# Attention outputs summed transposed on eight 64x32 tiles, expert weights in halves, and a reordered opening

## Chip, cores, metric

The kernel runs on one core of one Trainium2 chip. The metric is the device time of an execution in microseconds (us), given as the median of several executions. Each run belongs to a state (fast or slow, by its time against the fastest run of the same kernel), and comparisons here use fast runs unless a sentence says otherwise. A profile covers one execution; its span is some 1.7 us shorter than the device time.

PE is the tensor engine, PEld its weight loads, DVE the vector engine, ACT the scalar engine, POOL the general engine, SP the one that issues most transfers. PEclk is the clock granted to PE.

## The reference, cut to what matters

```python
def _attn_ref(r, k, v, w, u):                 # (4, 8, 768, 48): batch, heads, time, channels
    state = np.zeros((B, H, D, D))
    for t in range(S):
        cur = np.einsum('bhd,bhe->bhde', u[None] * kt, vt)
        y[:, :, t] = np.einsum('bhd,bhde->bhe', rt, state + cur)
        state = w[None, :, :, None] * state + np.einsum('bhd,bhe->bhde', kt, vt)

def _moe_ref(x, w_gate, w1, w2):              # x: (4, 768, 384), 8 experts, F = 1024
    logits = x.mean(axis=1) @ w_gate          # one expert for a whole sequence
    e_idx = np.argmax(logits, axis=1)
    ...
        h = np.maximum(x[mask] @ w1[e], 0.0)
        out[mask] = gate_w[mask, None, None] * (h @ w2[e])
```

A linear attention with a decaying state comes first. Its output, averaged over a sequence, chooses one expert for the sequence, so no expert work of a sequence can start before the attention of the whole sequence is done.

## The kernel before

Time is cut into blocks of 256 steps: three blocks a sequence, twelve in all (0 to 11). Within a block, scores are products of k and r, and outputs are products of masked scores (`gt`) and values (`vb`). Expert work is a queue of jobs (`hp` and `op` products), and `slot()` puts some of them between the pieces of attention. The opening does blocks 0 to 2 without expert work; the loop does blocks 3 to 11 with jobs of the sequence before.

The products that the change touches, in the shape they have before:

```python
# scores: four 64x64 tiles, 16 products for half of a block
nc.tensor.matmul(out=at[64 * j : 64 * j + 64, a, pp, cs, :],
                 lhsT=kt[q, p, j, cs, :], rhs=rt[q, p, j]..., start=True, stop=True)
...
# outputs: time on the partitions, one product of 48 columns for each head and half
nc.tensor.matmul(out=yj[:, D * h : D * h + D],
                 lhsT=gt[q, p // 2, a, p % 2, c, :], rhs=vb[q, c, h, :], ...)
...
def backs(g):     # outputs are copied, transposed back, and copied again; column sums for the gate
    nc.tensor.transpose(out=xv[:, ct, :, j, :], in_=xn[:, j, ct::NCT], identity=ident)
    nc.tensor.matmul(out=sp[:, o : o + 1], lhsT=xn[:, j, ct::NCT], rhs=ones_col, ...)
    nc.scalar.copy(xts[b][:, :, L * gi : L * gi + L], xp)
...
def weights(b):   # all of w1 in one transfer, then w2, when the gate has chosen
    nc.gpsimd.dma_start(out=w1..., in_=moe_w1[ds(ev, 1)]...)
```

The whole kernel:

## Time and profile before

| | before |
|---|---|
| time, median of the first three runs | 154.54 us (153.83 to 156.16) |
| span of the profiled run | 152.6 us |
| PE busy | 91% of the span |
| first gate logits (`lg`) | 33.1 us |
| first expert matmul (`hp`) | 45.0 us |

The prediction below shows the engine shares, the slices and the chain. Two lines that it did not look at also belong here. They are from the page's part on transfer queues; the columns are packets, MB, and share of the sixteen transfer engines' time:

```profile
q0 software_dynamic: 1152, 6.29, 22.3%
q8 instruction: 15, 0.25, 0.6%
```

I read queue 8 as PE's own program, by its packet count: 15 packets of 16 KB for the 3913 PE instructions of the trace, 261 to a packet. Queue 0 carries the expert weights.

### The profile page before, as it was taken

How to read it: one execution, taken by the hardware profiler on the slowest of the kernel's cores; microseconds unless marked ns; L12 is line 12 of the kernel's file. 1: busy time of each engine (PE TensorE's matmuls, PEld its weight loads, DVE VectorE, ACT ScalarE, POOL GpSimd, SP SyncE). 2: the span in 40 equal slices, each digit the busy share in tenths (PEclk: the TensorE clock that was granted, in tenths of full speed). 3: DMA queues.
4: the chain of work that ended last, by engine and by line, in shares of the span. 5: the costliest groups of instructions: out<-in, count | busy, mean ns of one | idle time of the engine just before them, and what ended most of it. 6: DMA issues, size and time to landing. Idle time of an engine off the chain costs nothing.

```text
span 152.6 us, 4539 instructions
## 1 busy us (share of the span) xinstructions
PE 139.5 (91%) x1951; PEld 97.9 (64%) x1951; DVE 74.4 (49%) x164; ACT 83.6 (55%) x144; POOL 68.5 (45%) x62
## 2 busy tenths in 40 slices
PE   6999877956989999999999999999999999999991
PEld 2266645644767878766677877666777765676560
DVE  7837796125465654754548456465562321121110
ACT  0976567351356766546476784563664543556231
POOL 4169659207976839289292862963021020000000
PEclk9999999995599999999999999999999999999999
DMA  2999998303999999999991000998020079960034
GB/s 59 301 322 321 279 268 226 99 0 92 227 215 297 249 312 269 293 214 210 215 376 48 4 0 4 153 195 267 22 93 4 0 111 208 161 247 0 0 126 185
DMA packets 41464, 25.47 MB, mean 167 GB/s; under 512 B 38755, under 2 KB 39012, under 8 KB 41444
## 3 DMA queue, kind: packets, MB, share of 16 engines
q1 hardware_dynamic: 39460, 18.89, 42.9%
q0 software_dynamic: 1152, 6.29, 22.3%
q8 instruction: 15, 0.25, 0.6%
q10 hardware_dynamic: 832, 0.00, 0.3%
q14 instruction: 5, 0.04, 0.1%
HBM read 26.76 MB, written 4.72 MB: 206 GB/s over the span
## 4 chain that ended last, share of the span: by engine, by line
PE 78%; DVE 10%; ACT 8%; issue 2%; DVEq 0%
PE op L503 21%; PE hp L483 21%; PE twp L236 7%; PE at L260 5%; DVE gt L268 5%; PE fill L113 5%; PE y L353 5%; ACT kr L246 4%; PE s L361 2%; PE xp L402 2%; ACT ht L490 2%; PE y L313 2%; PE y L323 2%; DVE ht L492 1%; DVE st L376 1%
## 5 line engine op out<-in xcount | busy, mean ns | idle before, releaser
L483 PE MATMUL hp<-xt,w 128*128 128x384 bf16 x192 | 41.4, 334 | 1.3 <-DVE lg L436 0.3
L503 PE MATMUL op<-w,ht 128*128 128x384 bf16 x192 | 34.9, 326 | 0.1
L246 ACT COPY kr<-twp 128x1024 bf16<-128x1024 bf16 x24 | 24.1, 1011 | 18.4 <-PE twp L236 18.4
L268 DVE TENSOR_TENSOR gt<-at,mask 128x1024 bf16<-128x1024 f32 x24 | 29.3, 1221 | 8.8 <-PE at L260 8.6
L490 ACT ACTIVATE ht<-hp 128x384 bf16<-128x384 f32 x48 | 23.4, 491 | 17.8 <-PE hp L483 17.1
L483 PEld LDWEIGHTS <-w 128*128 128x128 bf16 x192 | 25.0, 148 | 8.1 <-issue 4.4
L305 POOL TENSOR_TENSOR vt<-vb,tcol 128x768 bf16<-128x768 bf16 x11 | 16.3, 1477 | 25.4 <-DVE tcol L297 25.4
L503 PEld LDWEIGHTS <-ht 128*128 128x128 bf16 x192 | 17.3, 97 | 11.1 <-issue 0.8
L247 DVE TENSOR_TENSOR prod<-twp,kr 128x512 bf16<-128x512 bf16 x24 | 10.2, 424 | 27.8 <-ACT kr L246 27.8
L199 POOL TENSOR_TENSOR kp<-k,dk 128x768 bf16<-128x768 f32 x11 | 20.0, 1816 | 1.4 <-DMA k<-in_k_dram 1.4
L199 POOL TENSOR_TENSOR rp<-r,dr 128x768 bf16<-128x768 f32 x11 | 20.0, 1820 | 0.0
L510 ACT ACTIVATE ob<-op,gw 128x384 f32<-128x384 f32 x16 | 9.3, 581 | 13.2 <-PE op L503 12.9
L113 PE MATMUL fill<-zero 128*128 128x512 bf16 (+1 forms) x45 | 14.5, 430 | 1.9 <-DVE zero L85 1.3
L353 PEld LDWEIGHTS <-gt 64*128 64x128 bf16 x384 | 11.5, 94 | 5.0 <-issue 3.9
L492 DVE TENSOR_SCALAR ht<-hp 128x384 bf16<-128x384 f32 x16 | 8.9, 554 | 11.7 <-PE hp L483 11.5
L353 PE MATMUL y<-vb,gt 64*128 64x48 bf16 x384 | 14.1, 182 | 0.4 <-ACT xn L389 0.4
L260 PE MATMUL at<-kr 48*64 48x128 bf16 x384 | 10.5, 229 | 3.6 <-ACT kr L246 1.7
L389 ACT CAST xn<-y 128x384 bf16<-128x384 f32 x24 | 11.1, 480 | 4.1 <-PE y L323 3.5
L462 POOL DMA_DIRECT2D w<-in_moe_w_dram x4 | 2.5, 623 | 22.5 <-DVE gw L452 7.8
L260 PEld LDWEIGHTS <-kr 48*64 48x64 bf16 x384 | 7.0, 110 | 8.2 <-issue 6.2
L410 ACT COPY xt<-xp 128x768 bf16<-128x768 bf16 x12 | 9.6, 798 | 4.3 <-PE xp L402 4.3
L361 PE MATMUL s<-vb,kp 64*128 64x96 bf16 x160 | 10.5, 208 | 0.4 <-DVE st L376 0.4
(73 smaller groups left out, 155.6 us busy)
## 6 DMA issues: line engine op xcount, KB each, us to landing
w<-in_moe_w_dram POOLq DMA_DIRECT2D x8, 768.0 KB, 10.2
k<-in_k_dram SPq DMA_DIRECT2D x12, 384.0 KB, 5.1
r<-in_r_dram SPq DMA_DIRECT2D x12, 384.0 KB, 5.8
v<-in_v_dram SPq DMA_DIRECT2D x12, 384.0 KB, 5.7
out_dram<-ob SPq DMA_DIRECT2D x11, 384.0 KB, 5.6
out_dram<-ob SPq DMA_DIRECT2D x2, 192.0 KB, 1.9
wuT<-in_w_dram ACTq DMA_DIRECT2D x2, 0.8 KB, 3.6
wuT<-in_u_dram ACTq DMA_DIRECT2D x2, 0.8 KB, 4.1
```

The source lines that it names most:

```text
L113: nc.tensor.matmul(out=fills[-1][:, 0:cols], lhsT=zero[:, 0:128], rhs=zero[:, 0:cols], start=True, stop=True)
L199: eng.tensor_mul(dst[:, cs, :, 0:D].rearrange("q c h d -> q h c d"), src[:, :, cs, :], dec[:, :, cs, :])
L246: nc.scalar.copy(kts[g][:, :, :, c, :], tw)
L260: nc.tensor.matmul(out=at[64 * j : 64 * j + 64, a, pp, cs, :], lhsT=kt[q, p, j, cs, :], rhs=rt[q, p, j].rearrange("q c i -> q (c i)"), sta ...
L268: nc.vector.tensor_mul(gts[g][:, rnd].rearrange("q a p c t -> q (a p) c t"), at.rearrange("q a p c t -> q (a p) c t"), mask.rearrange("q n ...
L305: nc.gpsimd.tensor_mul(vt, vbs[g].rearrange("q c h d -> q (c h) d"), tcol.to_broadcast([128, 2 * H, D]))
L353: nc.tensor.matmul(out=yj[:, D * h : D * h + D], lhsT=gt[q, p // 2, a, p % 2, c, :], rhs=vb[q, c, h, :], start=(first and i == 0), stop=(c ...
L361: nc.tensor.matmul(out=sp[:, 96 * p : 96 * p + 96], lhsT=kp[g % NR][qo, c, 2 * p : 2 * p + 2, :].rearrange("s a b -> s (a b)"), rhs=vb[qo, ...
L389: nc.scalar.copy(xns[g][:, j, :], ys[g][j][:, 0:DM])
L483: nc.tensor.matmul(out=hp[:, 0:SB], lhsT=w1[:, ct, ft::NFT], rhs=xts[b][:, ct, SB * sb : SB * sb + SB], start=(ct == 0), stop=(ct == NCT - 1),
L490: nc.scalar.activation(out=o, in_=hp[:, 0:SB], func=ACT.Relu)
L503: nc.tensor.matmul(out=op[:, 0:DM], lhsT=ht[:, ft, 128 * si : 128 * si + 128], rhs=w2[:, ft, :], start=(ft == 0), stop=(ft == NFT - 1),)
```

## The change

The intent is to take work off PE and off the chain from attention to gate. Outputs are summed with channels on the partitions, where the expert products want them, so the copy, the back-transposes and the second copy go away. To keep PE's array filled with products of 32 output rows, eight tiles of 64 rows by 32 columns are meant to work side by side (in the trace of before, four score products on four tiles start within about 10 ns, and the next four 56 ns after the first). The gate's sums become products with the gate's weights. Each expert's w1 comes as two halves, and the opening is reordered.

```diff
 scores:
-                for j in range(2):
-                    for a in range(2):
-                        nc.tensor.matmul(out=at[64 * j : 64 * j + 64, a, pp, cs, :],
-                                         lhsT=kt[q, p, j, cs, :], ...)
+                for ih in range(2):
+                    for j in range(2):
+                        for a in range(2):
+                            o = 64 * j + 32 * ih
+                            nc.tensor.matmul(out=at[o : o + 32, a, pp, cs, :],
+                                             lhsT=kt[q, p, j, cs, 32 * ih : 32 * ih + 32], ...)
 ...
 outputs, a product for each 32 channels (u) of a window of 64:
+            nc.tensor.matmul(
+                out=y_slice(ys[g][j], G), lhsT=vb[q, c, o : o + 32],
+                rhs=gts[g][q, p // 2, a, p % 2, c, :], ...)
 ...
 state, two products of 32 rows (dh) for each head and half:
+            nc.tensor.matmul(
+                out=s_ps[g // NB][o : o + 32, 64 * p : 64 * p + 64],
+                lhsT=kp[g % NR][q, c, h, 32 * dh : 32 * dh + 32], ...)
 ...
+        together(row0, row1)        # rows of products interleaved, one of each in turn
+        nc.tensor.drain()
 ...
-                nc.tensor.transpose(out=xv[:, ct, :, j, :], in_=xn[:, j, ct::NCT], identity=ident)
 ...
 weights:
+        for fh in range(2):
+            nc.gpsimd.dma_start(out=t, in_=moe_w1[...][:, :, HF * fh : HF * fh + HF])
 ...
 opening:
+    wbc ... nc.sync.dma_start(out=wbc, in_=w...partition_broadcast(128))
+    load(0, "kr")
+    load(1, "kr")
 ...
-                nc.scalar.dma_start(out=wuT[...], ...)
+                nc.sync.dma_start(out=wuT[...], ...)      # now behind k and r of blocks 0 and 1
+    transposes(0, 1, nc.vector)
 ...
+    bonus(3)
+    prep_k(4)                       # POOL scales block 4 after the bonus of block 3
+    prep_r(4)
```

## The prediction

> **What bounds the kernel now.** I read the page first (engine shares, slices, chain by engine), then the groups with shapes kept apart, then the timeline of the tensor engine inside one block, and last the chain in order of time for the opening.
>
> ```profile
> PE 139.5 (91%) x1951; PEld 97.9 (64%) x1951; DVE 74.4 (49%) x164; ACT 83.6 (55%) x144; POOL 68.5 (45%) x62
> PE   6999877956989999999999999999999999999991
> PEclk9999999995599999999999999999999999999999
> PE 78%; DVE 10%; ACT 8%; issue 2%; DVEq 0%
> ```
>
> From slice 12 (about 45 us) on, PE is at 9 tenths in every slice; before that there are holes and two slices at half clock. So there are two regimes: an **opening** (0 to 45 us) bound by a chain over several engines, and a **loop and tail** (45 to 152.6 us) bound by PE. The engines beside PE are at half load.
>
> ```profile
> L483 PE MATMUL hp<-xt,w 128*128 128x384 bf16 x192 | 41.4, 334 | 1.3 <-DVE lg L436 0.3
> L503 PE MATMUL op<-w,ht 128*128 128x384 bf16 x192 | 34.9, 326 | 0.1
> L353 PE MATMUL y<-vb,gt 64*128 64x48 bf16 x384 | 14.1, 182 | 0.4 <-ACT xn L389 0.4
> L260 PE MATMUL at<-kr 48*64 48x128 bf16 x384 | 10.5, 229 | 3.6 <-ACT kr L246 1.7
> L402 PE MATMUL xp<-ident,xn 128*128 128x128 bf16 x72 | 6.5, 221 | 0.3
> L431 PE MATMUL lgp<-wg,pooled 128*128 128x8 f32 x24 | 3.2, 254 | 0.2 <-DVE pooled L420 0.2
> ```
>
> The mean duration of a matmul (182 to 334 ns) is not its cost, since they are pipelined. Cost is the distance between starts, which I take from the timeline. The expert matmuls stand 0.163 us apart (48 of them in 7.82 us on the chain at 123.53), so all 384 cost 62.4 us whatever the change does. What is left to win in the loop is the attention's share of PE.
>
> ```profile
> 78.49 0.33 PE L313 MATMUL y<-st,kr 128*128 128x96 bf16 x4
> ...
> 79.26 0.36 PE L323 MATMUL y<-vt,ident 64*64 64x384 bf16 x4
> 79.55 0.71 PE L483 MATMUL hp<-xt,w 128*128 128x384 bf16 x3
> 80.09 0.33 PE L313 MATMUL y<-st,kr 128*128 128x96 bf16 x4
> 80.36 0.42 PE L260 MATMUL at<-kr 48*64 48x128 bf16 x16
> 80.71 0.71 PE L483 MATMUL hp<-xt,w 128*128 128x384 bf16 x3
> ```
>
> Here the starts give the price of each piece: the four state products take 80.09 to 80.36, the 16 score products 80.36 to 80.71. The records also show that the score products start four at a time (four 64x64 tiles), 56 ns from group to group, and that their last start is 144 ns before the next 128x128 load: some 90 ns are lost when the tile shape changes, on the way in as well as out, and the first full matmul after it takes about 60 ns longer.
>
> ```profile
> 28.91 0.49 ACT xn L389
> ...
> 30.21 0.81 ACT xt L410
> 31.06 0.62 PE twp L236 x8
> 31.71 1.02 ACT kr L246
> 32.75 0.42 DVE prod L247
> 33.28 0.18 DVE top L438
> ...
> 45.11 0.64 PE hp L483 x3
> ```
>
> This is the end of the opening: after the last sum of block 2 the output goes through a copy (xn), transposes, a second copy (xt), and the gate's answer comes only at 33.3; the first expert matmul follows near 45 us.
>
> [...] The trace shows 64-column loads in the score products starting about 53 ns before the matmuls that need them, and hidden behind the previous group[...]. [...] 48-column products on one row group stand 25 ns apart, 96-column ones 42 ns, 128-column transposes 55 ns. [...]
>
> **The change, part by part.**
>
> *Attention on PE, per block of the loop, before.* From the starts: transposes 2x0.447 = 0.89; scores 2x0.35 = 0.70; bonus column 0.20; carried state 0.26; outputs with state 2x0.50 = 1.00; inter 2x0.264 = 0.53; bonus sum 0.29; back-transposes 0.34 and their column sums 0.16; four slow first matmuls 4x0.06 = 0.24. Sum 4.6 us. A sequence's first block has no carried state and one inter less: 4.1. Mean 4.4.
>
> *The same, after.* Instructions go from 129 pairs of load and matmul to 303. Outputs become 64 products of 128 columns, the bonus 48 of 64, inter 32 of 128, state 64 of 64, scores 64 of 128, on eight 64x32 tiles; the back-transposes go (0.34) and six short logit products replace the column sums (6x25 ns = 0.15). At 56 ns per 128 columns[...] on one tile, matmuls starting in order: scores 4 groups of 8, 0.23 each half. The first part has 16 output products, which do not spread evenly over the four column tiles (neighbouring heads share one 32-row group, so two of every four meet), some 7x56 ns, and state behind them: 0.47. The second part: 32 output products at the same imbalance 0.73,[...] inter 2x56 = 0.11, the last states alone some 0.15: 1.2 in all. Then the explicit drain, which I put at 0.25 (a matmul's 0.18 to 0.2 plus the restart), and the crossed inter 0.14. Only two changes of tile shape per block instead of four to five: 4x0.09 and 2x0.06 in and out, 0.48. Add transposes 0.89, carried 0.11, bonus column 0.20, logits 0.15: the sum is 0.46+0.47+1.2+0.25+0.14+0.48+0.89+0.11+0.20+0.15 = 4.35, and 4.2 for a first block; mean about 4.3. So smaller tiles buy little by themselves: what the extra products and the drain cost is about what the back-transposes and the saved shape changes give. Eight blocks: 8x0.15 = 1.2 us.
>
> *Gate.* Six fp32 matmuls (0.77 us a time) become one (about 0.3): three gates in the loop, 3x0.47 = 1.4 us.
>
> *Opening.* Decay by broadcast and the early table load start the decays about 1 us sooner; but k of block 0 then lands 0.6 us later (196 KB more ahead of it; before it landed at 5.0). Splitting block 0's copies over ACT and DVE brings its scores from 10.9 to about 10.0. The products on POOL, 1.82 us each, still pace blocks 1 and 2 (last one before ends at 16.3; the bonus weights have moved into that row), so block 1 gains nothing. Through blocks 1 and 2 each output loses a copy and transposes (about 1.5 us on the chain); I walk to the last sum of block 2 at 27.2 instead of 28.9. Then copies on two engines 0.6, logits 0.3, reduction, one matmul, copy: the gate's logits at about 29 instead of 33.1, **4 us sooner**. But most of this is given back: block 3 has one transpose buffer (0.45+1.0+0.42 per half, serial), its bonus product on POOL now stands before k and r of block 4 (1.5+1.8+1.8 us), and the first expert job comes after block 4's second transposes. I get about 12.5 us to block 4's first transposes and 14.5 to the first expert job: 43.6 instead of 45.0, with about 2.4 us more of block 3 left to do. The halves of w1 are no gain here (w1 landed at 43.5, 8.2 us after its trigger, before it was needed); they guard the later batches, whose jobs run some three jobs earlier.
>
> *Sum.* Before: from 45.04 to the last matmul at 149.3, 104.1 us = 62.4 expert + 37.5 attention and gates + 4.2 waits. After: attention left = 2.4 + 8x4.27 - 1.3 (no next block at the end) + 3x0.3 = 36.2; with the same 4.2 of waits 102.8; 43.6+102.8+3.5 (last copy and store) = 149.9 of span against 152.6. That is 2.7 us less: 154.54 becomes **about 151.8**. ACT loses 0.8 us per block and the tail three jobs, whose copies PE waits for today (48 hp products take 9.3 us at 132 where 7.8 would do): worth up to 1 us more. I predict **150.7**.
>
> **The rivals.** (a) *Dispatch becomes the bound.* In the loop PE now takes 158 pairs per 9.4 us block; after, 332. The longest dense run of the trace, 80 loads and matmuls in 0.70 us, is 8.8 ns each[...]; 400 in 8.9 us is the best long run. At 8 ns a pair the second part goes from 1.2 to 1.5 us; at 14 ns a pair to 2.2, and each block costs some 1.5 us more: 12 us in all, 160 and over. Against it: nothing in the trace shows dispatch as a wait in dense parts, and the rows are interleaved as if this had been tried. I give it one in ten for more than 2%. (b) *The opening gives nothing back.* If block 4's scaling fits into POOL's holes and the first expert job comes 3 us sooner than I walked, the time is near 147.5. The reordering is fine-grained enough to suggest that it was measured. (c) *A wait for weights.* The gate falls a few jobs before the queue of jobs is empty; w1 took 6.4 to 9.0 us from trigger to landing. If the half is not there in time, each of two batches loses 1 to 1.5 us: 153.5.
>
> **Range and chances.** The walk gives 151.8, the tail and ACT pull it to 150.7, (b) lies 3 us below, (c) 3 above, (a) far above. Range 146 to 155.5. The limit for faster is 151.4: I give 0.56 to faster, 0.34 to within 2%, 0.10 to slower.
>
> **What would show it right or wrong.** The page after should have about 3800 to 4000 matmuls; first hp near 43 to 44; lg of the first gate near 29; score products starting eight per 56 ns; the second part with its drain near 1.6 us between its first product and the next scores; no xn and xp rows. Wrong if the second part takes 2.5 us or more (rival a), if the first hp comes before 41 (rival b), or if hp shows waits for w of over 1 us (rival c).

Passages of this text are cut, as no trace of this case shows what they said. One of them takes a term out of the forecast's sum: the bonus products of the second part, 0.17 us, rested on a price for 64 columns that the trace of before does not have. The recorded sums stand as they came to with it: 1.2 us for the second part, 4.35 us per block, 149.9 us of span and 150.7 us of time. Without the cut term the block comes to 4.18, and eight blocks to some 1.4 us less. The states' part in the 0.47 and the 0.15 for the last states are estimates. The trace of before has no long run of pairs on eight tiles, so their rate was not shown.

## The result, and the profile after

| | before | after |
|---|---|---|
| time, median of four runs | 154.56 us (153.83 to 156.16) | 197.88 us (197.06 to 198.69) |
| span of the profiled run | 152.6 us | 196.3 us |
| granted clock, mean | 0.98 | 0.87 |
| PE instructions in the trace (loads and matmuls) | 3913 | 7746 |
| first `lg` / first `hp` | 33.1 / 45.0 us | 44.9 / 60.8 us |

The ratio is 1.282, with a 95% interval from 1.274 to 1.290: the change makes the kernel 28% slower. Ratios here are the mean time of one kernel's fast runs over that of the other's in the same rounds, so they are not quite the ratios of the medians.

The page of the kernel after, in the places that answer to the prediction's first fence (engine shares; PE and granted clock over 40 slices of 4.9 us; the chain that ended last by engine):

```profile
PE 143.0 (73%) x3861; PEld 96.3 (49%) x3863; DVE 72.3 (37%) x154; ACT 73.0 (37%) x126; POOL 75.8 (39%) x75
PE   7484448655347586999827968899874997948993
PEclk9969555785557999799985999999999699999999
PE 59%; issue 15%; DVE 8%; DMA 7%; ACT 5%; POOL 3%; SPq 0%; POOLq 0%; DVEq 0%
```

PE's busy time hardly rose (139.5 to 143.0 us), though the span grew by 43.7 us. So almost all of the added time is time in which PE stands still. "issue" is time in which PE waited for nothing that the profile shows. It went from 2% to 15% of the chain, that is from about 3 to about 30 us. The clock row shows a second difference: slices at half clock, many of them in the opening. The trace's clock record has 51.2 us at half clock in sum, against 6.8 us before.

Groups of instructions after (line, engine, operation, output and input, partitions by columns of the tile, matmul size, count; then busy us, mean ns, and idle time just before with its main cause):

```profile
L541 PE MATMUL hp<-xt,w 128*128 128x384 bf16 x192 | 42.5, 352 | 4.1 <-DMA w<-in_moe_w_dram 2.5
L561 PE MATMUL op<-w,ht 128*128 128x384 bf16 x192 | 35.2, 330 | 0.2
L337 PE MATMUL y<-gt,vb 64*32 64x128 bf16 x768 | 18.7, 234 | 3.9 <-issue 3.4
L356 PE MATMUL y<-kr,st 64*32 64x128 bf16 x320 | 11.2, 231 | 10.8 <-issue 9.9
L371 PE MATMUL y<-ident,vt 64*32 64x64 bf16 x576 | 12.0, 201 | 3.1 <-issue 3.1
```

The expert rows are as before. The holes stand in front of the small tiles and carry no releaser: 9.9, 3.4 and 3.1 us of "issue". The piece of the timeline with the longest hole (start, us, then what PE ran, with the idle time before it in brackets):

```profile
98.88 0.42 PE L388 MATMUL s<-vb,kp 64*32 64x64 bf16 x25
99.48 0.23 PE L356 MATMUL y<-kr,st 64*32 64x128 bf16 x3 [0.17 <-issue]
104.08 0.30 PE L356 MATMUL y<-kr,st 64*32 64x128 bf16 x4 [4.37 <-issue]
```

A row of products of one line stops for 4.37 us between its third and fourth member, with no wait that the profile shows, and then goes on. What makes the stops regular is their position in PE's instruction stream. I numbered PE's records (loads and matmuls) in order of start and looked at every 256th, with the offset that collects the most idle time. Position, time in us and the distance to the next start (usually 4 ns), where it is over 1 us:

```
 447  17.2  2.4 |  703  21.6  3.2 | 1215  33.3  1.9 | 1727  40.9  1.6 | 2239  62.5  2.0
2495  67.5  1.7 | 3007  75.5  2.0 | 4287  99.5  4.6 | 4799 114.9  1.5 | 6335 141.7  2.1
6847 149.7  2.1
```

Of 29 such boundaries, 18 show over 0.15 us, 28.7 us in sum: 9.3 us before the first gate logits and 19.4 us after them. The kernel before, counted at the same positions (to within three instructions), has at most 0.5 us in sum. The queue part of the page says what happens every 256 instructions:

```profile
q0 software_dynamic: 4288, 6.29, 18.9%
q8 instruction: 30, 0.49, 1.1%
```

PE's program now comes in 30 packets instead of 15. In 17 of the 18 stops, PE goes on 1.2 to 1.8 us after the end of such a packet. In the trace of after, a quiet round runs like this: PE enters a block at 38.96, the packet with the next one starts at 40.10 and takes 1.13, PE goes on at 42.52. That is 3.6 us from block to block. Beside bulk loads it is longer, since the packet starts later: entered at 19.59, packet at 22.54, on at 24.89, 5.3 us. Over the stops of this trace beside bulk loads, the distance from block to block is 4.6 to 6.5 us (143.7 to 148.3, and about 137.2 to 143.7), with one exception at 3.9 (31.3 to 35.2).

There are two further differences. The chain that ended last, in order of time (start, us, what), has them beside the stops:

```profile
17.41 2.18 issue
...
22.93 1.97 issue
...
33.60 1.63 issue
...
53.76 1.79 POOL kp L199
55.55 1.77 POOL rp L199
...
167.69 7.04 DMA w<-in_moe_w_dram
```

POOL's two products for block 4 now stand in front of everything between the gate and the first job, and late in the run the chain goes through a wait for expert weights. So there are three candidates: instruction fetch (the arrival of PE's own program), the order of the opening, and the weights.

### The profile page after: what moved, and what is told of

It reads as the page before. It is cut to its first block, busy times and chain, and to the rows that moved or that the text cites. A ratio compares the mean times of both kernels' runs of the same rounds, so it can differ in the third digit from the quotient of the medians.

```text
span 196.3 us, 8353 instructions
## 1 busy us (share of the span) xinstructions
PE 143.0 (73%) x3861; PEld 96.3 (49%) x3863; DVE 72.3 (37%) x154; ACT 73.0 (37%) x126; POOL 75.8 (39%) x75
## 3 DMA queue, kind: packets, MB, share of 16 engines
q0 software_dynamic: 4288, 6.29, 18.9%
## 4 chain that ended last, share of the span: by engine, by line
PE 59%; issue 15%; DVE 8%; DMA 7%; ACT 5%; POOL 3%; SPq 0%; POOLq 0%; DVEq 0%
PE hp L541 15%; PE op L561 13%; PE twp L235 6%; PE y L337 6%; PE at L268 5%; PE y L356 4%; DVE gt L276 4%; DMA w<-in_moe_w_dram 4%; DMA r<-in_r_dram 3%; PE s L388 3%; ACT ht L548 2%; PE y L371 2%; ACT kr L249 2%; PE fill L120 1%; PE s L472 1%
## 5 line engine op out<-in xcount | busy, mean ns | idle before, releaser
L561 PE MATMUL op<-w,ht 128*128 128x384 bf16 x192 | 35.2, 330 | 0.2
L541 PEld LDWEIGHTS <-w 128*128 128x128 bf16 x192 | 20.1, 118 | 14.8 <-issue 6.2
L464 ACT CAST xt<-y 128x384 bf16<-128x384 f32 x23 | 10.3, 480 | 39.5 <-PE y L356 29.7
L337 PE MATMUL y<-gt,vb 64*32 64x128 bf16 x768 | 18.7, 234 | 3.9 <-issue 3.4
L356 PE MATMUL y<-kr,st 64*32 64x128 bf16 x320 | 11.2, 231 | 10.8 <-issue 9.9
L235 PE MATMUL twp<-ident,kp 128*128 128x128 bf16 x96 | 10.9, 245 | 7.4 <-POOL kp L199 4.1
L337 PEld LDWEIGHTS <-vb 64*32 64x32 bf16 x768 | 13.8, 96 | 4.9 <-issue 4.9
L550 DVE TENSOR_SCALAR ht<-hp 128x384 bf16<-128x384 f32 x16 | 8.9, 553 | 19.4 <-PE hp L541 19.4
L268 PE MATMUL at<-kr 64*32 64x128 bf16 x768 | 12.9, 247 | 3.1 <-DVE gt L276 1.7
L518 POOL DMA_DIRECT2D w<-in_moe_w_dram x8 | 6.4, 805 | 22.3 <-DVE gw L505 22.3
L388 PE MATMUL s<-vb,kp 64*32 64x64 bf16 x640 | 13.1, 205 | 1.8 <-issue 1.8
L371 PE MATMUL y<-ident,vt 64*32 64x64 bf16 x576 | 12.0, 201 | 3.1 <-issue 3.1
(68 smaller groups left out, 153.3 us busy)
```

The costliest lines, as they stand in the source:

```text
L235: nc.tensor.transpose(out=twp[:, o + p, :], in_=src[:, c, 2 * p : 2 * p + 2, :].rearrange("s a b -> s (a b)"), identity=ident,)
L268: nc.tensor.matmul(out=at[o : o + 32, a, pp, cs, :], lhsT=kt[q, p, j, cs, 32 * ih : 32 * ih + 32], rhs=rt[q, p, j].rearrange("q c i -> q ( ...
L337: nc.tensor.matmul(out=y_slice(ys[g][j], G), lhsT=vb[q, c, o : o + 32], rhs=gts[g][q, p // 2, a, p % 2, c, :], start=first(g, j, G), stop= ...
L356: nc.tensor.matmul(out=y_slice(ys[g][j], G), lhsT=sts[g, j][q, p, 32 * u : 32 * u + 32], rhs=rts[g][q, p, j].rearrange("q c i -> q (c i)") ...
L388: nc.tensor.matmul(out=s_ps[g // NB][o : o + 32, 64 * p : 64 * p + 64], lhsT=kp[g % NR][q, c, h, 32 * dh : 32 * dh + 32], rhs=vb[q, c, win ...
L541: nc.tensor.matmul(out=hp[:, 0:SB], lhsT=w1[ft // 4][:, ct, ft % 4 :: 4], rhs=xts[b][:, ct, SB * sb : SB * sb + SB], start=(ct == 0), stop ...
```

## The experiments

All runs were compared with the kernel before on the same chip, where its median was 154.57 to 154.68 us.

**1. The suspected cost alone (m_fetch, a single run).** A kernel with nothing else in it: two dense runs of 1280 pairs of load and matmul on eight 64x32 tiles, the second while 4.7 MB are written, then wide matmuls with bare loads between. Its output is zeros, wrong.

```diff
+    pairs(0, a, 160)                        # 160 groups of eight pairs
+    for b in range(2): nc.sync.dma_start(out=out[...], in_=big[...])
+    pairs(1, m[1], 160)
+    for n in range(24):
+        wide(m[3], 4)
+        for _ in range(16): nc.tensor.ldweights(a[:, 0:128])
```

> A stream of the tensor engine by itself, no attention and no experts (its result is wrong on purpose). Stretch 1: 1280 pairs of weight load and matmul on eight 64x32 tiles, 64 columns each, with no bulk transfer. Stretch 2: the same while 4.7 MB are written out. Stretch 3: sixteen bare weight loads for every four wide matmuls. The theory (instructions arrive in blocks of 256 and a block takes about 3.6 us to come when the transfer engines are quiet, 4.6 to 6.5 us when they are busy): stretch 1 starves at every 256th instruction, at about 3.6 us per block, so 2560 instructions take about 33 us[...], and stretch 2 takes 4.5 us or more per block while the writes last. The rival (eight small tiles and their weight loads are slow themselves): an even pace with no gaps at block ends, the same in both stretches.[...]

It took 126.54 us. The chain and two groups of its page:

```profile
PE 55%; issue 43%; DVE 1%; DVEq 0%
L46 PE MATMUL p<-a,m 64*32 64x64 bf16 x1280 | 12.7, 225 | 24.9 <-issue 24.9
L46 PE MATMUL p<-a 64*32 64x64 bf16 x1280 | 12.6, 221 | 22.2 <-issue 22.2
```

PE stopped at every 256th instruction of the dense runs, for 2.4 to 2.95 us when the other transfers were quiet. PE needs about 1.05 us for 256 such instructions (4 ns each), and blocks follow each other every 3.45 to 4.0 us. The first stop comes at PE's 449th record. Beside the write, one stop was 6.03 us (block to block 7.1). 18 of 21 boundaries show a stop; the other three follow blocks with wide matmuls, which last 8 us and more. The instruction queue moved 22 packets, and in all 18 stops PE went on 1.2 to 1.6 us after one of them had ended. So it is the arrival of instructions that PE waits for. The rival, that small tiles are issued slowly but evenly, is half right: within a block eight pairs take 67 ns, at full and at half clock alike. But that is 1.05 us of the 3.45 to 4.0 us of a block; the rest is the stop.

**2. Fewer other transfers (a_noloads, a single run).** The kernel after, in which blocks 7 to 11 use the k, r and v of earlier blocks again (wrong).

```diff
+            if g > 6:
+                raw[name, g] = kept[name, g - 4]
+                continue
```

> The changed kernel without the loads of k, r and v for blocks 7 to 11 (it works on older blocks; wrong on purpose). Instructions and tiles stay as they are. The theory of instruction blocks: a block comes in about 3.6 us where it took 4.6 to 6.5 beside a load, so the starved time of the loop (about 18 us of the 28) falls by 6 to 10 us and the whole to some 188 to 192 us. The rival that small tiles, changes of tile shape or the drain cost the time: nothing moves, 197 us, as the loads were never waited for by the attention of those blocks.

It took 193.54 us, from 197.88. The idle time at boundaries fell from 28.7 to 21.1 us. At two boundaries that lost their neighbouring loads (2239 and 2495), the stops of 2.0 and 1.7 us became 0.4 and 0.3; the longest grew from 4.6 to 5.5. The direction is as expected, the gain smaller: 7.6 us of idle time bought 4.3 us, perhaps because part of it had stood beside other waits (not shown). So bulk loads lengthen the fetch but are not its main part.

**3. Fewer instructions (a_fewer).** The kernel after, with the same transposed outputs, opening and halves, but scores and state on 64x64 tiles and bonus on 64x128. The result is correct. Some rows of products stand one after the other instead of interleaved.

```diff
-                for ih in range(2):
-                    ...
-                                out=at[o : o + 32, a, pp, cs, :],
+                        nc.tensor.matmul(
+                            out=at[64 * j : 64 * j + 64, a, pp, cs, :],
 ...
-                lhsT=vt[q, c, 32 * G : 32 * G + 32], rhs=ident[q, q],
+                lhsT=vt[q, c, 128 * ct : 128 * ct + 128], rhs=ident[q, q],
 ...
-                lhsT=kp[g % NR][q, c, h, 32 * dh : 32 * dh + 32],
+                lhsT=kp[g % NR][q, c, h, :],
```

> The changed kernel with fewer, larger matmuls for the same sums: scores on 64x64 tiles (32 pairs a block, not 64), state on 64x64 (32, not 64), bonus on 64x128 (12, not 48). That is 200 instructions fewer per block of sequence, and some four more changes of tile shape per block, 0.09 us each. The theory of instruction blocks: fewer boundaries fall into dense stretches; 2300 instructions fewer are nine blocks fewer, starved time 28 us falls to about 8 to 12, so about 178 to 184 us. The rival that eight 64x32 tiles are good and only the opening went wrong: it gets slower by some 4 us, 201 us. The rival that the small tiles are slow by themselves[...]: it gains too, but without gaps at every 256th instruction, and the gaps at block ends stay as they are.

The median is 175.18 us, below the expected 178 to 184, and the ratio is 1.130 (1.119 to 1.141). PE instructions went from 7746 to 5476, idle time at boundaries from 28.7 to 2.95 us (2.47 of it at one boundary). The mean of the fast runs fell by 23.0 us, from 197.9 to 174.8 (one of the four runs was slow). From its page, the chain by engine and the instruction queue:

```profile
PE 60%; DMA 12%; DVE 11%; issue 5%; ACT 5%; POOL 4%; POOLq 1%; SPq 0%; DVEq 0%
q8 instruction: 21, 0.34, 0.8%
```

"issue" is back at 5%, and transfers (8 of the 12 points are expert weights) have become the next wait. A second pair of runs of the same kernel gave 174.66 us (one fast run at 173.25, one slow):

> This one is the earlier version with fewer instructions, run again as the yardstick beside the early weights of the next run on the same chip: 174 to 178 us.

**4. More instructions where they can be afforded (b_scores).** The reverse test: the kernel before with its scores alone on eight 64x32 tiles.

```diff
-                for j in range(2):
-                    ...
-                            out=at[64 * j : 64 * j + 64, a, pp, cs, :],
+                for ih in range(2):
+                    ...
+                                out=at[o : o + 32, a, pp, cs, :],
```

> The kernel before with its score products alone on eight 64x32 tiles (768 instead of 384, so 768 PE instructions more, 3913 to 4681). Fetch theory: a block of 256 instructions then lasts 6 to 6.5 us on average, still longer than the fetch of 3.6 us except right after a dense stretch: starvation under 4 us and 154 to 158 us. Rival, that 64x32 tiles are themselves slow on PE (each costs more than its share): 24 stretches of 32 more products at 25 ns or more each are 19 us, over 165 us.

(The rival's 25 ns is the spacing of the 48-column products in the trace of before.) The median is 154.12 us, ratio 0.998 (0.991 to 1.005): the same. The trace has 4677 PE instructions, and the idle time at boundaries, counted at the same positions, is 0.2 us. Its PE slices and instruction queue:

```profile
PE   6989767956989999999999999999999999999991
q8 instruction: 18, 0.29, 0.8%
```

So 64x32 tiles do not make a kernel slow by themselves, and 764 more instructions are free here. What differs is how long a block of 256 lasts. Between first job and last attention block, the time from one boundary to the next is:

| kernel | PE instructions | shortest / median time of a block of 256 | idle at boundaries, whole run | time |
|---|---|---|---|---|
| before | 3913 | 7.4 / 7.9 us | 0.3 us | 154.6 us |
| b_scores | 4677 | 5.0 / 6.4 us | 0.2 us | 154.1 us |
| a_fewer | 5476 | 3.0 / 5.4 us | 3.0 us | 175.2 us |
| after | 7746 | 2.4 / 5.1 us | 28.7 us | 197.9 us |

In the last row the blocks include the stops, so without them their median would be shorter. The cost works like a threshold: nothing as long as a block lasts longer than a fetch (3.45 to 4.0 us quiet, 4.6 to 6.5 beside loads), and about the difference for each block that does not (in m_fetch 1.05 us of work in a block of 3.45 to 4.0 us, and stops of 2.4 to 2.95). It is not sharp: two blocks of the kernel after were followed after 2.4 and 3.2 us, and one of a_fewer after 3.0 us with a stop of only 0.16. There the packet had started 0.6 us or less after PE's entry (in a_fewer just before it), not 1.1.

**5. Earlier weights (a_early).** The rival says that late weights are the cause. Here expert 0's weights are loaded before the gate has answered, so no job waits for them. The numbers are wrong.

```diff
+    load_w(0)                     # in the opening, after load(5)
 ...
+        if gi == 0:
+            load_w(b)             # at the first block of a sequence, not after its gate
-        ev = nc.gpsimd.value_load(idx8[0:1, 0:1], min_val=0, max_val=E - 1)
```

> The changed kernel, but the weights are always those of expert 0 and are loaded before the gate has answered (wrong on purpose where the gate chooses another). Fetch theory: PE's starvation stays near 28 us, and only what PE waited for weights goes, about 5 to 7 us (7 us of DMA w stand on the chain, and 2.5 us before hp): 190 to 194 us against 198. Rival, that late weights are the main cause and the stillness at instruction boundaries only fills time that PE would wait anyway: below 180 us.

The median is 199.78 us, ratio 1.288 (1.280 to 1.296): nothing gained. The row of the expert products shows that the wait is gone:

```profile
L545 PE MATMUL hp<-xt,w 128*128 128x384 bf16 x192 | 44.3, 359 | 1.1 <-DVE ht L554 0.6
```

Idle time before `hp` went from 4.1 to 1.1 us, but the stops at boundaries rose from 28.7 to 31.0, apparently since the transfers moved to where other blocks are fetched (the one near 67 us, now beside a load of w1, grew from 1.7 to 3.6). Late weights are therefore not the main cause, and my expected gain of 4 to 8 us failed too: a wait taken away here was given back.

**6. The order on POOL (a_order).** The kernel after, with POOL scaling block 4 ahead of the bonus product of block 3.

```diff
     prep_v(3)
+    prep_k(4)
+    prep_r(4)
 ...
     bonus(3)
-    prep_k(4)
-    prep_r(4)
```

> The changed kernel with the scaling of k and r of block 4 placed on POOL ahead of the bonus of block 3 rather than behind it. In the profile the tensor engine waits 4.2 and 1.5 us for that scaling (51.4 to 57.4). If the order on POOL is the cause of that wait, the first expert matmul comes 4 to 5 us sooner (56 instead of 61.0) and the whole is 193 to 195 us. If starved instructions hide behind it, less than 2 us come of it.

The first `hp` came at 57.9 instead of 60.8 us, and the median is 196.01 us, ratio 1.259 (1.244 to 1.275). So the order costs 2.9 us at that place. In the end the three fast runs have a mean of 195.4 us against 197.9, a gain of 2.5 us that is hardly clear of noise (the two intervals touch at 1.274).

**7. The opening alone (b_open).** The kernel before, with the new order of loads, the broadcast decay, the early table load and the second engine for block 0.

```diff
-    nc.sync.dma_start(out=wrow, in_=w...)
+    nc.sync.dma_start(out=wbc, in_=w...partition_broadcast(128))
+    load(0, "kr")
+    load(1, "kr")
-                nc.scalar.dma_start(out=wuT[...], ...)
+                nc.sync.dma_start(out=wuT[...], ...)
 ...
-    transposes(0, 1)
+    transposes(0, 1, nc.vector)
```

> The kernel before with only the opening of the change: decay by a broadcast load, table load first, k and r of blocks 0 and 1 ahead of v, the small columns on the same queue, block 0's second copy on DVE. As predicted, the split and the early decays bring block 0 to its scores near 10.0 instead of 10.9 us and the whole is within 1% of before, perhaps 1 us less. As the changed kernel's profile reads (r of block 0 landed at 8.4 us there, 6.5 us before; the broadcast row at 5.5), block 0 starts 1 to 1.5 us later and the whole is 155 to 156 us. Neither can account for the 16 us by which the first expert matmul moved: the first hp should stay between 44 and 47 us.

One of its four runs was fast, at 156.75 us; the others, the profiled one among them, took 159.4 to 159.6, so no ratio is given. In the profiled (slow) run the first `hp` came at 50.2 us, outside the expected 44 to 47. Its longest wait for these constants (engine, line, who releases it: us in total, times, longest):

```profile
POOL U L177 <- DMA wuT<-in_u_dram: 8.1, 1, 8.1
```

The small decay and bonus columns now stand behind 1.5 MB of k and r on one queue, and POOL waits 8.1 us for them before it scales block 1. In the kernel after, the product that needs them had been moved later, so this wait is partly a fault of my transplant. The opening brings no gain here, but what it costs in the kernel after is not settled by this run.

**8. Halves alone (b_halves).** The kernel before with w1 in two halves.

```diff
-            in_=moe_w1[ds(ev, 1)].rearrange("o (p ct) f -> p (o ct f)", ct=NCT))
+                in_=moe_w1[ds(ev, 1)].rearrange("o (p ct) f -> p (o ct) f", ct=NCT)[
+                    :, :, HF * fh : HF * fh + HF])
```

> The kernel before with only the expert weights in halves (w1 in two loads of 2 KB rows, w2 in two runs per partition). If halves bring the first half sooner, as the change intends, it lands some 4 us after its trigger, where the whole w1 took 6.4 to 9.0. If the cost lies in the number of packets, the half lands 6 to 7 us after its trigger as in the changed kernel and w2 2 to 3 us later than now. The time stays within 1% in both cases, since the kernel before has some 10 us of expert work in hand when a gate is decided.

The median is 154.83 us, ratio 1.004 (0.997 to 1.011): the same. The first halves landed 5.4 to 7.1 us after their trigger, against 6.4 to 9.0 for a whole w1 before, and w2 landed at 49.7 instead of 47.5 us in the first batch. Packets on the weights' queue rise from 1152 to 4288, as in the kernel after. The halves neither help nor hurt.

**9. What is left, put together (c_best, c_early).** c_best is a_fewer with before's opening of constants, logits of block 0 later, POOL scaling block 4 early, w1 whole and jobs starting later in the loop (correct). c_early is c_best with expert 0's weights loaded early, as in run 5 (wrong).

```diff
-    wbc ... partition_broadcast(128)
+    wrow ... wps (before's product with ones)
-        for fh in range(2): ...
+        w1 = wpool.tile([128, NCT, F], BF16, tag="w1", name=f"w1_{b}")
+    prep_k(4)
+    prep_r(4)
     scores(2, 1)
+    logits(0)
 ...
         evac_x(g)
+        acc[1] = True
```

> The version with fewer matmuls, and in addition: the opening of the kernel before (row and matmul for the decay, columns from ACT's queue), the first logits later in program order, POOL's scaling of block 4 ahead of the first gate, w1 as a whole, and the expert jobs starting after the fifth slot. The version with fewer matmuls took 175 us, of which the profile gives 6.6 and 7.4 us on the chain to waits for w, 2 us to the gate's constants and 5 us to POOL's scaling of block 4. If these are what is left, it comes to 156 to 162 us, the first hp near 46 to 48 us; if small tiles cost more than the profile shows, it stays above 168.

> The version with fewer instructions, the opening of before and later expert jobs, with expert 0's weights loaded ahead of the gate (wrong on purpose). If what was left there over before (12 us) is mostly the wait for weights (11 percent of its chain), it falls by 4 to 8 us, to 160 to 164 us. If it is the opening (first hp 5 us later than before) and the slower clock after it, it stays at 166 or above.

c_best took 167.84 us, ratio 1.076 (1.066 to 1.085), and c_early 164.48 us, ratio 1.061 (1.053 to 1.069). The expected 156 to 162 us for c_best was missed. The first `hp` came at 49.9 and 49.6 us, still almost 5 us later than before. Fast runs alone have a mean of 166.5 and 164.5 us, so the weights are worth some 2 us there, less than expected and not clear of noise (the intervals overlap). In c_early, 5.0 us of stops at boundaries remain, as does a clock of 0.93 against 0.98. The fetch is gone as the main cost, and the transposed outputs still do not beat the kernel before.

**10. An attempt to beat both (b_best).** The kernel before, with k and r of block 1 loaded ahead of v, POOL scaling block 4 ahead of the gate, and the gate ahead of block 3's transposes.

```diff
+    load(0, "kr")
+    load(1, "kr")
+    load(0, "v")
+    load(1, "v")
 ...
-    transposes(3, 0)
-    gate(0)
-    weights(0)
     prep_r(4)
     prep_v(4)
+    gate(0)
+    weights(0)
+    transposes(3, 0)
```

> The kernel before with three moves and no other change: k and r of block 1 loaded ahead of the v's, POOL's scaling of block 4 ahead of the first gate, and the first gate ahead of block 3's transposes. POOL waited until 9.2 us for k of block 1 and paces blocks 1 and 2, so about 1 us less in the opening, and r of block 4 is scaled 36.6 to 38.4 us now, which holds its transposes back by 0.5 to 1 us. About 152.5 to 153.5 us, 1% faster; if the opening is bound by ACT and DVE alone, within 0.3% of before.

The median of six is 155.09 us, ratio 0.993 (0.985 to 1.000), which is the same. Its three fast runs took 153.3 to 154.1. Before has two levels as well, near 154.4 and 156.1, so the difference between the lower levels is about 0.7 us, and the other three runs of b_best, at 156.1 to 156.6, lie no lower than before's upper level. No version here clearly beats the kernel before.

## Why the prediction was wrong

The predicted span of 149.9 us was 43.6 to the first expert matmul, 102.8 from there to the last matmul and 3.5 for the rest. The trace has 60.8, 132.1 and 3.4.

**The step that failed** is the price of the attention on PE after the change. "Instructions go from 129 pairs of load and matmul to 303" was counted, and then each block was priced by the time that its columns occupy tiles, 4.35 us against 4.6: the instructions themselves cost nothing in that sum. Dense stretches in a trace that never starves cannot show the price of an instruction. What the runs put in its place is a price by blocks of 256: a fetch of about 3.6 us quiet and 4.6 to 6.5 us beside loads. The kernel after has 332 pairs, or 664 instructions, per loop block by the prediction's own count. If such a block took the predicted 9.4 us or so, 256 instructions would last 3.6 us on average (256 / 664 x 9.4, an estimate), about as long as a quiet fetch, and in the dense second part far less.

**Rival (a)** named the right place, "400 in 8.9 us is the best long run", and got one chance in ten. Its mechanism was half right: it took an even pace of 8 or 14 ns a pair. m_fetch shows 8.3 ns a pair within a block, its lower figure, which by the prediction's own sum costs 0.3 us a block (1.2 to 1.5). The stops between blocks, which are the main cost, it did not have. It also took the smallness of dispatch waits in the kernel before as evidence against it, where blocks last 7.4 us or more and cannot show it.

**The unstarved costs were right.** From the first output product of the second part to the next block's scores, the prediction had 1.6 us. Measured from start to start it is 1.5, 1.5 and 1.6 us in the three blocks of the loop without a stop there (87.13 to 88.62 is one). In the other five it is between 3.2 and 7.2 us, past the 2.5 at which the prediction called itself wrong. The 32 score products start within 0.20 to 0.36 us in all groups of the loop but two, where 0.23 was predicted; 3861 matmuls lie in the 3800 to 4000, and a drain shows 0.27 to 0.40 us where 0.25 was put.

**The opening** was to bring the gate's logits at about 29 us; they came at 44.9. Five stops of 9.3 us in sum lie before that, and four of them stand in the chain as "issue", 7.1 us in all. The 12.5 us from there to block 4's first transposes hold: those of k start 10.7 us later (55.61) and those of r 12.5 us later (57.37), behind the bonus product and both scalings on POOL, as told; the first expert job came 1.4 us later than the 14.5 that were put. Of the 15.9 us by which the logits came late, the 6.6 that are not stops are not taken apart run by run: the wait for POOL's gate constants is 2.4 us of it in the waits view, and r of block 0 landed at 8.4 instead of 6.5 us.

**The halves** were called "no gain here", which b_halves confirms. **Rival (c)** came true in its sign, with a wait of 2.5 us before `hp`, but a_early shows that removing it gains nothing in a kernel whose PE is starved (199.78 us against 197.88).

**The clock** was not priced in the prediction. Slices at half clock go with PE's holes: in the kernel after, PE stood for 4.4 us from 99.7 us on, and the clock record has half clock from 101.9 to 108.7 us. Shorter stops go with it too: in m_fetch the clock was at half from 15.8 to 46.6 us, and no stop in that time was longer than 2.96 us (PE stood for 2.4 to 2.96 us of every 3.45 to 4.0). What sets the clock was not shown. How many of the 43 us are due to it alone is open; no run held the clock constant.

**The sum**, by means of the fast runs. Of 43.1 us, 23.0 go when the instruction count goes to 5476 and 25.8 us of stops with it; this is shown, with the reservation that a_fewer also has fewer interleaved rows. c_best takes off another 8.3 us by the opening's order, the later jobs and the whole w1 together, not each by itself. c_early takes off some 2 by weights. About 10 us remain and go with the later first job (4.6 us), the remaining stops (5.0 us in sum) and the clock; these may overlap and are not separated.

## What to carry to other kernels

Count the instructions of an engine per unit of time as well as its work: when 256 of them take less time than a fetch (here about 3.6 us, or 4.6 to 6.5 beside bulk loads), smaller pieces are paid for in whole microseconds. Where 256 take longer, the added pieces cost nothing here (764 of them in b_scores, ratio 0.998). Holes without a releaser are worth numbering by their position in the instruction stream before any other theory is tried, and the packets of the instruction queue tell how many blocks there are. A trace with slack cannot price the resource that has it; a micro kernel that uses only that resource can.
